# The run-out of an attention and adapter kernel, reordered: banks, additions and the branch at the end

## The chip, the cores and the metric

The kernel runs on one core of one Trainium2 chip. Its time is that of one execution on the device, in microseconds. The median of three runs of the kernel before the change is 412.86 us, the lowest 411.19 and the highest 413.30.

A core has five engines with an instruction stream each. TensorE (PE in the profile, PEld for its weight loads) multiplies matrices into PSUM. VectorE (DVE) and ScalarE (ACT) read PSUM and SBUF. GpSimd (POOL) works here on SBUF operands alone. SyncE (SP) issues transfers. Each engine runs its instructions strictly in the order of the program, and engines wait for one another by semaphores. Transfers can be issued from SP's, ScalarE's and GpSimd's queues.

## The reference

A spatial-reduction attention is followed by a mixture of low-rank adapters. Cut to what matters:

```python
# kv (4, 384, 32, 128), q (4, 12288, 128)
kv_pool = kv.reshape(B, H//4, 4, W//4, 4, C).mean(axis=(2, 4))   # 768 pooled rows per batch
k = v = kv_pool.reshape(B, -1, C) @ w_sr
a = softmax(q @ k.T / sqrt(C))
x = a @ v                                  # then seen as (49152, 128)

logits = x @ w_gate                        # 8 experts
topk = the two largest of the 8
w = softmax(logits[topk])
out = x + sum over the two of w * ((x @ A[e]) @ B[e])     # A: 128x16, B: 16x128
```

## The kernel before, in words

The 49152 tokens are cut into 96 chunks (`NCH`) of 512 tokens (`NTOK`), 24 chunks to each of the four batches. A chunk's tokens are handled as four groups (`NS`) of 128. The last chunk, 95, is called n in the code.

A chunk c goes through these helpers, each of which issues its instructions where it is called:

- `scores` (L231): on TensorE, 512 queries against two blocks of 128 keys, in a two-bank PSUM tile from the pool `ps_s` (`stile`, L147, two such tiles that take turns). ScalarE takes the exponential into `tt`. Three calls make a chunk.
- `weigh` (L242): the weighted sum of the values, 12 matmuls in each of two halves, into the two-bank tile `xps` of the pool `ps_x`, of which there is one. The value matrix has the 8 gate columns and a column of ones appended, so logits and the softmax's denominator come out with it.
- `normalise` (L253): on VectorE, a reciprocal, the multiplication that makes `xn` in SBUF and frees `xps`, and four searches for the largest logits.
- `gate` (L269) and `gate_weights` (L284): for a pair of chunks, the argument and the mask of the two best experts, and the weights by a tanh on ScalarE. The engine of the small multiplications and additions is a parameter, GpSimd or VectorE.
- `transposed` (L291): on TensorE, the transposes of x of one chunk (`cx`) and of the gated hidden values `hg` of an older one (`ch`) into one bank. It returns `evacuate`, which copies both to SBUF on VectorE or, with `True`, on ScalarE.
- `down` (L326): x times A into a bank `h_ps`. `apply_gate` (L332): on VectorE, `hg`, the product of it with the gate weights.
- `up` (L343): `hg` times B into a bank `d_ps`. With `plus_x` the same bank first takes x, by four fp32 matmuls with the identity (8 passes, L347).
- `give` (L353): VectorE adds `xn` to `d_ps` (L358), or, where x is in the bank already, ScalarE copies it (L356). Then the transfer of the 512 rows to the output is issued, from SP's queue unless another is named.

`mtile` takes a tile of the pool `ps_h`, which is one bank; `ps_t` is one bank too. With two for `ps_x` and four for `ps_s` all eight banks of PSUM are in use.

The order is written out by hand (`manual_schedule`). The main loop (L457) handles in its step c the scores of chunks c+1 and c+2, the weighted sum of c-1, the transposes of c-2 and c-4, `down` of c-3, and `up` and `give` of c-6. Pooling and keys of the next batch are spread over the steps (`prep`). From step 89 on, small pieces check that all values were in a safe range; `count_sum` (L394) adds up counts over partitions with a matmul into a bank of `ps_h`.

After the loop, from L505, comes the run-out for the chunks still on their way. The score pool is closed, and its four banks become the pool `ps_e`, named by `bank(0)` to `bank(3)`. The lines L511 to L557 are the order of the work there, each engine taking its own instructions out of it in that order. `tail_ok` (L401) and `all_ok` (L406) finish the check and leave a flag `bad`.

At the end each engine loads the flag into a register (`values_load`, L559), and an `If` (L562) holds a slow general version of the whole computation, which is not entered with these inputs. In the profile, L562 also names the waits for outstanding work that follow the branch, and L673 the closing steps of the program.

Of the kernel before, what the change touches and what calls it, by code (L numbers as in the profile page):

```python
# [21 lines left out]
def kernel(  # L22
# [44 lines left out]
    def mtile(shape, dtype=FP32, name="hd"):  # L67
        return ps_h.tile(shape, dtype, tag="hd", name=name)
# [78 lines left out]
    def stile(name):  # L147
        return ps_s.tile([P, 2, NTOK], FP32, tag="sg", name=name)
# [90 lines left out]
            mm(sg[:, k], kfT[b][:, j * P:(j + 1) * P], qc, start=True, stop=True)  # L239
        nc.scalar.activation(tt[c][:, 2 * r:2 * r + 2], sg, AF.Exp, bias=0.0, scale=scale)  # L240

    def weigh(c, h):  # L242
        b = c // CPB
        if h == 0:
            xps[c] = ps_x.tile([P, 2, 512], FP32, tag="x", name="xps")
        for j in range(h * NH, (h + 1) * NH):
            for s in range(NS):
                o = xps[c][:, s // 2, (s % 2) * VW:(s % 2 + 1) * VW]
                mm(o, tt[c][:, j, s::NS], vext[b][:, j],  # L249
                   start=(j == 0 and s % 2 == 0), stop=(j == NJ - 1 and s % 2 == 1),  # L250
                   skip_group_check=True)

    def normalise(c):  # L253
        ri = rinv_all[:, c]
        xv = xps[c][:, :, 0:2 * VW].rearrange("p b (s v) -> p b s v", v=VW)
        nc.vector.reciprocal(ri.rearrange("p (b s) -> p b s", b=2), xv[:, :, :, VW - 1])  # L256
        if c % 2 == 0:
            xpair[c // 2] = xpool.tile([P, 2 * NS, VW], FP32, tag="xn", name="xn")
        xn[c] = xpair[c // 2][:, (c % 2) * NS:(c % 2 + 1) * NS]
        nc.vector.tensor_tensor(  # L260
            xn[c].rearrange("p (b s) v -> p b s v", b=2), xv,
            ri.rearrange("p (b s) -> p b s", b=2).unsqueeze(3).broadcast_to([P, 2, 2, VW]),
            op=ALU.mult)
        if c % 2 == 0:
            gin[c // 2] = small.tile([P, 2 * NS, 8], FP32, tag="top", name="top")
        for s in range(NS):
            nc.vector.max(gin[c // 2][:, (c % 2) * NS + s], xn[c][:, s, C:C + E])  # L267
# [23 lines left out]
    def transposed(cx, ch, bank=None):  # L291

        if bank is None:
            t_ps = ps_t.tile([P, 2, NS, P], BF16, tag="tp", name="t_ps")
        else:
            t_ps = bank.bitcast(BF16).rearrange("p (k s c) -> p k s c", k=2, s=NS)
        todo = []
        if chunk_ok(cx):
            hi = xn[cx].bitcast(U16)[:, :, 1:2 * C:2].bitcast(BF16)
            todo += [(0, s, hi[:, s]) for s in range(NS)]  # L300
        if chunk_ok(ch):
            todo += [(1, s, hg[ch][:, s]) for s in range(NS)]
        if not todo:
            return lambda act=False: None
        for i, (k, s, src) in enumerate(todo):
            mm(t_ps[:, k, s], src, id_bf, is_transpose=True,  # L306
               start=(i == 0), stop=(i == len(todo) - 1), skip_group_check=True)

        def evacuate(act=False):
            xh = run.tile([P, 2, NS, P], BF16, tag="xh", name="xh", bufs=5)  # L310
            lo, hi_ = todo[0][0], todo[-1][0] + 1
            if act:
                nc.scalar.activation(xh[:, lo:hi_], t_ps[:, lo:hi_], AF.Copy)
            else:
                nc.vector.tensor_copy(xh[:, lo:hi_], t_ps[:, lo:hi_])  # L315
            if lo == 0:
                xT[cx] = xh[:, 0]
            if hi_ == 2:
                hgT[ch] = xh[:, 1]

        return evacuate

    def as_tokens(bank):
        return bank.rearrange("p (s c) -> p s c", s=NS)

    def down(c, bank=None):  # L326
        hps[c] = mtile([P, NS, P], name="h_ps") if bank is None else as_tokens(bank)
        for s in range(NS):
            mm(hps[c][:, s], xT[c][:, s], a_bf, start=(s == 0), stop=(s == NS - 1))  # L329
# [9 lines left out]

    dps = {}  # L340

    def up(c, bank=None, plus_x=False):

        dps[c] = mtile([P, NS, P], name="d_ps") if bank is None else as_tokens(bank)
        if plus_x:
            for s in range(NS):
                mm(dps[c][:, s], id_f32, xn[c][:, s, 0:C], start=(s == 0), stop=False,  # L347
                   skip_group_check=True)
        for s in range(NS):
            mm(dps[c][:, s], hgT[c][:, s], b_bf, start=(s == 0 and not plus_x),  # L350
               stop=(s == NS - 1), skip_group_check=True)

    def give(c, act=False, queue=None):  # L353
        osb = run.tile([P, NS, P], FP32, tag="osb", name="osb", bufs=8)
        if act:
            nc.scalar.activation(osb, dps[c], AF.Copy)  # L356
        else:
            nc.vector.tensor_tensor(osb, dps[c], xn[c][:, :, 0:C], op=ALU.add)  # L358
        t0 = c * NTOK
        (queue or nc.sync).dma_start(  # L360
            out[t0:t0 + NTOK, :].rearrange("(p s) c -> p s c", p=P), osb)
# [30 lines left out]
        nc.vector.tensor_scalar(flags[:, 2:], vmax, V_LO, None, op0=ALU.is_ge)  # L392

    def count_sum():  # L394
        cnt_ps = mtile([1, 2 + 2 * B], name="cnt_ps")
        mm(cnt_ps, ones_c, flags, start=True, stop=True)
        nc.vector.tensor_copy(cnt[:, 0:2], cnt_ps[:, 0:2])
        nc.vector.tensor_scalar(cnt[:, 2:], cnt_ps[:, 2:], 1.0, None, op0=ALU.min)  # L398
        nc.vector.tensor_reduce(tot, cnt, axis=AX.X, op=ALU.add)
# [57 lines left out]
    for c in range(1, NCH - 1):  # L457
        b, k = divmod(c, CPB)
        todo = [(c + 1, 2), (c + 2, 0), (c + 2, 1)]

        def next_scores():
            x, r = todo.pop(0)
            if x < NCH:
                scores(x, r)

        cs = c + 2
        if cs < NCH and cs % GRP == 0:
            g = cs // GRP
            if g + 2 < NQ:
                load_q(g + 2)  # L470
            if g + 3 < NQ:
                cast_q(g + 3)
        next_scores()
        if c >= 3 and c % 2 == 1:
            gate_weights((c - 3) // 2, nc.gpsimd)
        weigh(c - 1, 0)
        next_scores()
        if chunk_ok(c - 6):
            up(c - 6)
            give(c - 6)  # L480
        weigh(c - 1, 1)
        normalise(c - 1)
        if c % 2 == 0:
            gate(c // 2 - 1, nc.gpsimd)
        evacuate = transposed(c - 2, c - 4)
        next_scores()
        if b + 1 < B:
            prep(b + 1, k)
        if c == 1:
            ranges(0)  # L490
        a = slice(0, CUT * NS)
        if CUT < c <= CUT + 3:
            count_ok(a, c - CUT - 1, flags[:, 0:1])
        elif c == CUT + 4:
            values_ok()
        elif c == CUT + 5:
            count_sum()
        if chunk_ok(c - 3):
            down(c - 3)
            apply_gate(c - 3)  # L500
        evacuate(c == NCH - 2)
# [2 lines left out]

    score_banks.close()  # L505
    ps_e = ctx.enter_context(tc.tile_pool(name="ps_e", bufs=1, space=bass.MemoryType.PSUM))

    def bank(i):
        return ps_e.tile([P, NTOK], FP32, tag=f"e{i}", name=f"e{i}")

    n = NCH - 1  # L511
    gate_weights(n // 2 - 1, nc.gpsimd)
    weigh(n - 1, 0)
    weigh(n - 1, 1)
    normalise(n - 1)
    evacuate = transposed(n - 2, n - 4, bank(0))
    evacuate(True)
    down(n - 3, bank(1))
    apply_gate(n - 3)
    up(n - 6, bank(2))  # L520
    weigh(n, 0)
    weigh(n, 1)
    give(n - 6)
    normalise(n)
    tail_ok()
    gate(n // 2, nc.vector)
    evacuate = transposed(n - 1, n - 3)
    evacuate(True)
    down(n - 2)
    apply_gate(n - 2)  # L530
    up(n - 5, bank(3), plus_x=True)
    evac_x = transposed(n, NCH, bank(0))
    gate_weights(n // 2, nc.vector)
    evac_x(True)
    down(n - 1, bank(1))
    give(n - 5, act=True)
    up(n - 4, bank(2), plus_x=True)
    apply_gate(n - 1)
    evacuate = transposed(NCH, n - 2)
    evacuate(True)  # L540
    down(n)
    apply_gate(n)
    give(n - 4, act=True)
    end = ps_x.tile([P, 2, 512], FP32, tag="x", name="end")
    up(n - 3, end[:, 0], plus_x=True)
    give(n - 3, act=True)
    up(n - 2, bank(3), plus_x=True)
    evac_1 = transposed(NCH, n - 1, bank(0))
    evac_1()
    all_ok(bank(2))  # L550
    evac_2 = transposed(NCH, n, ps_t.tile([P, NTOK], FP32, tag="tp", name="t_ps"))
    evac_2()
    give(n - 2, act=True)
    up(n - 1, bank(1))
    give(n - 1, queue=nc.scalar)
    up(n)
    give(n, queue=nc.scalar)  # L557

    bad_v = nc.values_load(bad, min_val=0, max_val=1)  # L559


    with tc.If(bad_v != 0):  # L562
        b_full = const.tile([P, P], FP32)
        nc.vector.tensor_copy(b_full, b_f)
        big = kvpool.tile([P, 4 * 1024], FP32, tag="kvt", name="g_kv")
# [112 lines left out]
```

## Time and profile before

| | us |
|---|---|
| profiled execution, its own time | 412.09 |
| its span, from the first to the last instruction | 410.3 |
| median of three runs | 412.86 |
| TensorE busy | 380.0 |
| VectorE busy | 344.4 |
| ScalarE busy | 297.9 |
| GpSimd busy | 165.2 |
| end of the last computation (VectorE L358) | 403.73 |

All starts are counted from the start of the span. A busy TensorE is not TensorE at its peak, because matmuls overlap and their ends are modelled. The granted clock of TensorE has a mean of 0.991. The main loop's step takes 3.5 to 4.1 us near its end: step 94 is the stretch from 387.30 to 390.03 and the wait after it. The run-out's computation goes from 390.6 to 403.7.

A line of an engine's work has the line of the code, the engine, the operation, what is written from what, and the shape. "PEldq", "SPq" and the like are the sequencers of those engines, with the register, branch and issuing instructions that are not counted as busy. A chain is a list of pieces in order of time: start, length, and the engine and line that held up the end in that piece.

### The profile page before, as it was taken

The page shows a single profiled execution, that of the slowest core. Times are in us where ns is not written, and L with a number is a line of the kernel's source. Part 1 is how long each engine was busy: PE and PEld are TensorE (multiplying, and loading weights), DVE is VectorE, ACT ScalarE, POOL GpSimd, SP SyncE. Part 2 cuts the span into 40 slices and gives each one's busy share as a digit, 9 for nine tenths or more (in the row PEclk, how much of TensorE's full clock was granted, in tenths as well). Part 3 has the DMA queues.
Part 4 walks back from the last instruction along what each step waited for, and adds up shares of the span by engine and source line. Part 5 has one row for each costly group of instructions (what it writes and reads, how often), then busy time and mean ns, then how long its engine had stood idle before and what let it go on. Part 6 is the DMA issues. An engine that isn't in the chain of part 4 may idle for free.

```text
span 410.3 us, 11470 instructions
## 1 busy us (share of the span) xinstructions
PE 380.0 (93%) x4561; PEld 304.0 (74%) x4561; DVE 344.4 (84%) x969; ACT 297.9 (73%) x356; POOL 165.2 (40%) x315
## 2 busy tenths in 40 slices
PE   0659999999999999999999999989999999999992
PEld 0426888777877888877877888867878788787791
DVE  3663789898899989898899989898898989899982
ACT  1267888876687877876687878866777888877751
POOL 1020498882212487792212488692212212122120
PEclk9998999999999999999999999999999999999998
DMA  8999699797186999797186999797185474221123
GB/s 259 378 251 181 232 248 289 284 185 154 66 169 134 290 244 310 241 249 156 60 173 119 322 233 305 263 227 154 55 180 115 139 162 129 79 78 74 57 80 135
DMA packets 71372, 76.51 MB, mean 186 GB/s; under 512 B 51744, under 2 KB 52000, under 8 KB 70944
## 3 DMA queue, kind: packets, MB, share of 16 engines
q1 hardware_dynamic: 68816, 62.93, 55.1%
q0 software_dynamic: 736, 12.06, 16.8%
q10 hardware_dynamic: 1760, 0.73, 0.7%
q8 instruction: 37, 0.61, 0.6%
q14 instruction: 23, 0.19, 0.1%
HBM read 50.53 MB, written 37.22 MB: 214 GB/s over the span
## 4 chain that ended last, share of the span: by engine, by line
PE 79%; DMA 8%; DVE 7%; issue 2%; ACT 1%; ACTq 0%; SPq 0%; DVEq 0%; POOL 0%
PE xps L249 31%; PE sg L239 26%; PE t_ps L306 9%; PE d_ps L350 5%; PE h_ps L329 4%; DMA qT<-q_bf 3%; DMA b_f<-in_moe_B_dram 3%; DMA kvt<-in_kv_dram 2%; DVE xn L260 2%; DVE hg L334 2%; DMA q_bf<-in_q_dram 1%; PE v_ps L171 1%; PE k_ps L164 1%; DVE osb L358 1%; ACT tt L240 1%
## 5 line engine op out<-in xcount | busy, mean ns | idle before, releaser
L240 ACT ACTIVATE tt<-sg 128x1024 f16<-128x1024 f32 x288 | 282.6, 1022 | 75.8 <-PE sg L239 75.3
L239 PE MATMUL sg<-qT,kfT 128*128 128x512 bf16 x576 | 172.3, 382 | 2.4 <-ACT kfT L186 1.0
L249 PEld LDWEIGHTS <-tt 128*128 128x128 f16 x2304 | 154.6, 113 | 23.7 <-DVE xn L260 2.1
L249 PE MATMUL xps<-vext,tt 128*128 128x137 f16 x2304 | 170.9, 224 | 0.6 <-DVE xn L260 0.4
L358 DVE TENSOR_TENSOR osb<-d_ps,xn 128x512 f32<-128x512 f32 x90 | 62.1, 689 | 17.7 <-PE d_ps L350 14.3
L273 POOL TENSOR_TENSOR m<-top 128x8 f32<-128x8 f32 x47 | 10.9, 232 | 157.5 <-DVE top L267 157.2
L260 DVE TENSOR_TENSOR xn<-xps,rinv_all 128x548 f32<-128x548 f32 x96 | 69.9, 728 | 3.3
L140 POOL TENSOR_TENSOR kvt<-kvt 128x1024 f32<-128x1024 f32 x27 | 64.0, 2372 | 4.3 <-PE sg L239 1.9
L334 DVE TENSOR_TENSOR hg<-h_ps,gw 128x512 bf16<-128x512 f32 x94 | 63.8, 678 | 0.4 <-PE h_ps L329 0.4
L315 DVE COPY xh<-t_ps 128x1024 bf16<-128x1024 bf16 (+1 forms) x93 | 62.4, 671 | 0.0
L239 PEld LDWEIGHTS <-kfT 128*128 128x128 bf16 x576 | 45.3, 98 | 5.7 <-issue 2.3
L350 PEld LDWEIGHTS <-xh 128*128 128x128 bf16 x384 | 29.2, 98 | 25.8 <-issue 5.6
L329 PEld LDWEIGHTS <-xh 128*128 128x128 bf16 x384 | 29.2, 98 | 21.0 <-issue 0.7
L267 DVE MAX8 top<-xn 128x8 f32<-128x8 f32 x384 | 36.0, 156 | 3.3
L350 PE MATMUL d_ps<-b_bf,xh 128*128 128x128 bf16 x360 | 34.8, 219 | 3.2 <-DVE hg L334 2.9
L329 PE MATMUL h_ps<-a_bf,xh 128*128 128x128 bf16 x376 | 36.3, 219 | 0.6 <-DVE cnt L398 0.6
L306 PE MATMUL t_ps<-id_bf,hg 128*128 128x128 bf16 x376 | 36.3, 219 | 0.0
L306 PE MATMUL t_ps<-id_bf,xn 128*128 128x128 bf16 x376 | 36.3, 219 | 0.0
L288 POOL TENSOR_SCALAR th<-th 128x64 f32<-128x64 f32 x47 | 17.4, 370 | 37.4 <-ACT th L286 37.4
L256 DVE RECIPROCAL rinv_all<-xps 128x4 f32<-128x4 f32 x96 | 17.5, 183 | 14.4 <-PE xps L249 11.5
L306 PEld LDWEIGHTS <-xn 128*128 128x128 bf16 x384 | 26.0, 98 | 0.0
L306 PEld LDWEIGHTS <-hg 128*128 128x128 bf16 x384 | 25.4, 98 | 0.1
(96 smaller groups left out, 207.4 us busy)
## 6 DMA issues: line engine op xcount, KB each, us to landing
kvt<-in_kv_dram SPq DMA_DIRECT2D x48, 512.0 KB, 7.2
out_dram<-osb SPq DMA_DIRECT2D x94, 256.0 KB, 3.0
q_bf<-in_q_dram POOLq DMA_DIRECT2D x23, 512.0 KB, 6.3
out_dram<-osb ACTq DMA_DIRECT2D x2, 256.0 KB, 3.7
qT<-q_bf SPq DMA_TRANSPOSE x23, 6.7
w_in<-in_w_sr_dram ACTq DMA_DIRECT2D x1, 64.0 KB, 2.0
a_f<-in_moe_A_dram ACTq DMA_DIRECT2D x1, 64.0 KB, 9.6
b_f<-in_moe_B_dram ACTq DMA_DIRECT2D x1, 64.0 KB, 10.3
```

The costliest lines, as they stand in the source:

```text
L140: eng.tensor_tensor(v[:, 0], v[:, 0], v[:, d], op=ALU.add)
L239: mm(sg[:, k], kfT[b][:, j * P:(j + 1) * P], qc, start=True, stop=True)
L240: nc.scalar.activation(tt[c][:, 2 * r:2 * r + 2], sg, AF.Exp, bias=0.0, scale=scale)
L249: mm(o, tt[c][:, j, s::NS], vext[b][:, j], start=(j == 0 and s % 2 == 0), stop=(j == NJ - 1 and s % 2 == 1), skip_group_check=True)
L260: nc.vector.tensor_tensor(xn[c].rearrange("p (b s) v -> p b s v", b=2), xv, ri.rearrange("p (b s) -> p b s", b=2).unsqueeze(3).broadcast_t ...
L267: nc.vector.max(gin[c // 2][:, (c % 2) * NS + s], xn[c][:, s, C:C + E])
L306: mm(t_ps[:, k, s], src, id_bf, is_transpose=True, start=(i == 0), stop=(i == len(todo) - 1), skip_group_check=True)
L315: nc.vector.tensor_copy(xh[:, lo:hi_], t_ps[:, lo:hi_])
L329: mm(hps[c][:, s], xT[c][:, s], a_bf, start=(s == 0), stop=(s == NS - 1))
L334: nc.vector.tensor_tensor(hg[c].rearrange("p s (e r) -> p (s e) r", r=RK), hps[c].rearrange("p s (e r) -> p (s e) r", r=RK), g.rearrange(" ...
L350: mm(dps[c][:, s], hgT[c][:, s], b_bf, start=(s == 0 and not plus_x), stop=(s == NS - 1), skip_group_check=True)
L358: nc.vector.tensor_tensor(osb, dps[c], xn[c][:, :, 0:C], op=ALU.add)
```

## The change

The loop and the run-out are rewritten in these places:

- `weigh` can be given its PSUM tile. In the run-out chunk 94's sum (n-1) gets two of the closed score pool's banks, from a pool `ps_y`, which is closed after `normalise(n - 1)` and followed by `ps_f` with two banks. Chunk 95's sum (n) keeps `xps`.
- `up` loses `plus_x`; `x_first` puts x into a bank by fp32 matmuls and is called for n-2 alone. Four chunks did that before (n-5, n-4, n-3, n-2).
- `give` has three ways: `"add"` (VectorE, as before), `"copy"` (ScalarE, where x is in the bank) and `"pool"` (ScalarE copies, and GpSimd adds `xn` in place). `"pool"` is used for n-6, n-5, n-4 and n-3. n-6 is now done in the loop's step 94, with `d_ps` in a score bank; the transfer of each is issued from SP after the GpSimd addition.
- `count_sum` moves from step 93 to step 94 and uses a score bank.
- The order of the run-out differs. `gate(n // 2)` stays on VectorE and comes after the transposes of n-1, `gate_weights(n // 2)` goes from VectorE to GpSimd. `apply_gate(n)`, its transposes and `up(n)` come ahead of those of n-1. Output n is issued from SP; n-2 and n-1 from ScalarE's queue.
- The `If` names its false side as the block that is preferred next in the code.

```diff
--- before.py
+++ after.py
@@ -239,9 +239,11 @@
             mm(sg[:, k], kfT[b][:, j * P:(j + 1) * P], qc, start=True, stop=True)
         nc.scalar.activation(tt[c][:, 2 * r:2 * r + 2], sg, AF.Exp, bias=0.0, scale=scale)
 
-    def weigh(c, h):
+    def weigh(c, h, banks=None):
         b = c // CPB
-        if h == 0:
+        if banks is not None:
+            xps[c] = banks
+        elif h == 0:
             xps[c] = ps_x.tile([P, 2, 512], FP32, tag="x", name="xps")
         for j in range(h * NH, (h + 1) * NH):
             for s in range(NS):
@@ -339,23 +341,30 @@
 
     dps = {}
 
-    def up(c, bank=None, plus_x=False):
-
-        dps[c] = mtile([P, NS, P], name="d_ps") if bank is None else as_tokens(bank)
-        if plus_x:
-            for s in range(NS):
-                mm(dps[c][:, s], id_f32, xn[c][:, s, 0:C], start=(s == 0), stop=False,
-                   skip_group_check=True)
+    def x_first(c, bank):
+
+        dps[c] = as_tokens(bank)
         for s in range(NS):
-            mm(dps[c][:, s], hgT[c][:, s], b_bf, start=(s == 0 and not plus_x),
+            mm(dps[c][:, s], id_f32, xn[c][:, s, 0:C], start=(s == 0), stop=False,
+               skip_group_check=True)
+
+    def up(c, bank=None):
+        fresh = c not in dps
+        if fresh:
+            dps[c] = mtile([P, NS, P], name="d_ps") if bank is None else as_tokens(bank)
+        for s in range(NS):
+            mm(dps[c][:, s], hgT[c][:, s], b_bf, start=(s == 0 and fresh),
                stop=(s == NS - 1), skip_group_check=True)
 
-    def give(c, act=False, queue=None):
+    def give(c, how="add", queue=None):
+
         osb = run.tile([P, NS, P], FP32, tag="osb", name="osb", bufs=8)
-        if act:
+        if how == "add":
+            nc.vector.tensor_tensor(osb, dps[c], xn[c][:, :, 0:C], op=ALU.add)
+        else:
             nc.scalar.activation(osb, dps[c], AF.Copy)
-        else:
-            nc.vector.tensor_tensor(osb, dps[c], xn[c][:, :, 0:C], op=ALU.add)
+        if how == "pool":
+            nc.gpsimd.tensor_tensor(osb, osb, xn[c][:, :, 0:C], op=ALU.add)
         t0 = c * NTOK
         (queue or nc.sync).dma_start(
             out[t0:t0 + NTOK, :].rearrange("(p s) c -> p s c", p=P), osb)
@@ -392,7 +401,7 @@
         nc.vector.tensor_scalar(flags[:, 2:], vmax, V_LO, None, op0=ALU.is_ge)
 
     def count_sum():
-        cnt_ps = mtile([1, 2 + 2 * B], name="cnt_ps")
+        cnt_ps = stile("cnt_ps")[0:1, 0, 0:2 + 2 * B]
         mm(cnt_ps, ones_c, flags, start=True, stop=True)
         nc.vector.tensor_copy(cnt[:, 0:2], cnt_ps[:, 0:2])
         nc.vector.tensor_scalar(cnt[:, 2:], cnt_ps[:, 2:], 1.0, None, op0=ALU.min)
@@ -479,6 +488,9 @@
             up(c - 6)
             give(c - 6)
         weigh(c - 1, 1)
+        if c == NCH - 2:
+            up(c - 5, stile("d_ps")[:, 0])
+            give(c - 5, "pool")
         normalise(c - 1)
         if c % 2 == 0:
             gate(c // 2 - 1, nc.gpsimd)
@@ -493,7 +505,7 @@
             count_ok(a, c - CUT - 1, flags[:, 0:1])
         elif c == CUT + 4:
             values_ok()
-        elif c == CUT + 5:
+        elif c == CUT + 6:
             count_sum()
         if chunk_ok(c - 3):
             down(c - 3)
@@ -504,62 +516,72 @@
 
     score_banks.close()
     ps_e = ctx.enter_context(tc.tile_pool(name="ps_e", bufs=1, space=bass.MemoryType.PSUM))
+    x_banks = ExitStack()
+    ps_y = x_banks.enter_context(tc.tile_pool(name="ps_y", bufs=1, space=bass.MemoryType.PSUM))
 
     def bank(i):
         return ps_e.tile([P, NTOK], FP32, tag=f"e{i}", name=f"e{i}")
 
+    def t_bank():
+        return ps_t.tile([P, NTOK], FP32, tag="tp", name="t_ps")
+
     n = NCH - 1
     gate_weights(n // 2 - 1, nc.gpsimd)
-    weigh(n - 1, 0)
+    weigh(n - 1, 0, ps_y.tile([P, 2, 512], FP32, tag="y", name="xps"))
     weigh(n - 1, 1)
     normalise(n - 1)
+    x_banks.close()
+    ps_f = ctx.enter_context(tc.tile_pool(name="ps_f", bufs=1, space=bass.MemoryType.PSUM))
+
+    def fbank(i):
+        return ps_f.tile([P, NTOK], FP32, tag=f"f{i}", name=f"f{i}")
+
     evacuate = transposed(n - 2, n - 4, bank(0))
     evacuate(True)
     down(n - 3, bank(1))
     apply_gate(n - 3)
-    up(n - 6, bank(2))
+    up(n - 5)
+    give(n - 5, "pool")
     weigh(n, 0)
     weigh(n, 1)
-    give(n - 6)
     normalise(n)
     tail_ok()
-    gate(n // 2, nc.vector)
     evacuate = transposed(n - 1, n - 3)
     evacuate(True)
     down(n - 2)
+    gate(n // 2, nc.vector)
+    evac_x = transposed(n, NCH, fbank(0))
+    evac_x(True)
+    end = ps_x.tile([P, 2, 512], FP32, tag="x", name="end")
+    x_first(n - 2, end[:, 0])
+    up(n - 4, bank(1))
     apply_gate(n - 2)
-    up(n - 5, bank(3), plus_x=True)
-    evac_x = transposed(n, NCH, bank(0))
-    gate_weights(n // 2, nc.vector)
-    evac_x(True)
-    down(n - 1, bank(1))
-    give(n - 5, act=True)
-    up(n - 4, bank(2), plus_x=True)
-    apply_gate(n - 1)
+    gate_weights(n // 2, nc.gpsimd)
+    down(n - 1, fbank(1))
+    give(n - 4, "pool")
+    down(n, fbank(0))
     evacuate = transposed(NCH, n - 2)
     evacuate(True)
-    down(n)
     apply_gate(n)
-    give(n - 4, act=True)
-    end = ps_x.tile([P, 2, 512], FP32, tag="x", name="end")
-    up(n - 3, end[:, 0], plus_x=True)
-    give(n - 3, act=True)
-    up(n - 2, bank(3), plus_x=True)
-    evac_1 = transposed(NCH, n - 1, bank(0))
-    evac_1()
-    all_ok(bank(2))
-    evac_2 = transposed(NCH, n, ps_t.tile([P, NTOK], FP32, tag="tp", name="t_ps"))
-    evac_2()
-    give(n - 2, act=True)
-    up(n - 1, bank(1))
+    up(n - 3, bank(0))
+    apply_gate(n - 1)
+    evac_0 = transposed(NCH, n, t_bank())
+    evac_0()
+    up(n - 2)
+    all_ok(mtile([P, NTOK], name="okc"))
+    give(n - 3, "pool")
+    evac_1 = transposed(NCH, n - 1, fbank(1))
+    evac_1(True)
+    up(n, fbank(0))
+    give(n)
+    give(n - 2, "copy", queue=nc.scalar)
+    up(n - 1)
     give(n - 1, queue=nc.scalar)
-    up(n)
-    give(n, queue=nc.scalar)
 
     bad_v = nc.values_load(bad, min_val=0, max_val=1)
 
 
-    with tc.If(bad_v != 0):
+    with tc.If(bad_v != 0, preferred_fallthrough_block=False):
         b_full = const.tile([P, P], FP32)
         nc.vector.tensor_copy(b_full, b_f)
         big = kvpool.tile([P, 4 * 1024], FP32, tag="kvt", name="g_kv")
```

## The prediction

> **What bounds the kernel now.** I read the page first, then the chain of the work that ended last, cut to the end, then what follows the last computation.
>
> ```profile
> span 410.3 us, 11470 instructions
> PE 380.0 (93%) x4561; PEld 304.0 (74%) x4561; DVE 344.4 (84%) x969; ACT 297.9 (73%) x356; POOL 165.2 (40%) x315
> ```
>
> TensorE bounds the long middle, which the change leaves as it is up to chunk 93. The change can only move what lies after about 386 us. There the chain reads (start, length, what):
>
> ```profile
> 386.90 0.04 DVE cnt L397
> 386.94 0.08 DVE cnt L398
> 387.02 0.05 issue
> 387.07 0.40 PE h_ps L329 x4
> ...
> 389.83 0.74 DVE xn L260
> 390.57 0.04 issue
> 390.62 1.66 PE xps L249 x24
> ...
> 395.62 0.95 PE e L347 x8
> ...
> 401.45 0.42 DVE xh L315
> ...
> 402.46 0.68 DVE osb L358
> ```
>
> Three things are to be seen. At 387 TensorE waits for the copies out of cnt_ps. At 390.62 and again at 393.30 the weighted sums wait for VectorE to empty their one PSUM tile. From 394.95 to 401.43 the chain never leaves TensorE, and four groups like the one at 395.62 (x added by fp32 matmuls, 0.95 us each) are in it.
>
> The computation ends at 403.73, and the span 6.6 us later. Four views tell why: the branch of the If (line 562) by engine, the output transfers issued from 397 to 403 us and those issued from 403 to 404.5, and the DMA rate in forty slices of 401.5 to 407 us.
>
> ```profile
> L562 PEldq COMPARE_BRANCH  x1: 4394/4394/4394, 403.4 to 403.4; - x1
> L562 SPq COMPARE_BRANCH  x1: 58/58/58, 403.1 to 403.1; - x1
> ```
> ```profile
> DMA to landing us min/median/max: 2.0/2.0/2.0
> ```
> ```profile
> DMA to landing us min/median/max: 3.2/3.7/4.2
> ```
> ```profile
> GB/s 313 387 357 402 357 90 0 0 104 402 357 402 357 268 15 0 0 60 149 372 387 298 387 328 417 417 492 268 119 60 30 60 60 119 30 15 0 15 0 15
> ```
>
> Outputs land in 2.0 us, but the last two in 3.2 and 4.2. Their data moved at about 400 GB/s until about 405.2, and then a trickle went on for 2 us. Counted by DMA engine, 12 of the 16 shares of the last output had landed by 405.88 and the sixteenth only at 407.96. In that time the instruction queues fetched five blocks of code, one of them 16 KB with 1.26 us on a single engine. TensorE's branch needed 4.4 us, the others' under 0.1 (and some 0.45 to their next instruction). SP waits for the sixteenth share at 407.96 and the span ends 2.35 us after it; TensorE was through at 408.05 and is not last.
>
> **The base.** The profiled execution took 412.09 us, 1.8 more than its span and 0.2% under the 412.86 median; I subtract from the median.
>
> **The change, step by step.** n is chunk 95. Durations are rows of this trace: 4 bf16 matmuls 0.22 us of TensorE's chain, a full weighted sum 1.48, four fp32 additions of x 0.95; 0.2 from the last issue to the reader; VectorE hg 0.68, xn 0.73, osb 0.67; ScalarE 1.02 for a 1024-wide copy, 0.59 for 512.
>
> The count (count_sum) goes to chunk 94's step and into a score bank. Its TensorE wait of 0.56 at 387.07 and about 0.3 of its own go from step 93; chunk 93's second half ends 0.8 us sooner, at 388.61. In step 94 it costs 0.2 on TensorE and 0.4 on VectorE ahead of hg(91).
>
> New in step 94: up(89), 0.22 on TensorE until 388.83; a ScalarE copy until 389.63; a GpSimd add. A GpSimd add of this shape has a row:
>
> ```profile
> L144 POOL TENSOR_TENSOR kvt<-kvt x9: 1275/1284/1290, 59.7 to 274.7; 128x512 f32<-128x512 f32 x9
> ```
>
> So it ends at 390.94. Queued behind it on GpSimd is the gate of chunks 92 and 93, ready only at 390.2; it starts at 390.97 (391.05 before). On SP the output of 89 leaves at 391 instead of 394.9, with nothing pending behind it.
>
> Chunk 94's sum gets its own banks. If these are the ones of up(89), they are free at 389.63, and TensorE, there at 389.72, goes on to 391.20. If they were those of the count, it would wait for VectorE until 390.8, 1.05 more. I take the first, since the score buffers alternate and an even number of takes comes before the last score.
>
> VectorE then has count, hg(91) to 391.48, recip and xn(94) to 392.43, hg(92) to 393.72. TensorE: transposes to 391.75, down(92), up(90), and chunk 95's sum from 392.19 to 393.67 (394.95 before). xn(95) is done at 394.83 (395.94 before).
>
> From here VectorE's gate ends at 395.97 and the tanh at 396.3. The two gate multiplications move to GpSimd: 0.37 and 0.32 with 0.08 ahead of each, to 397.16, where VectorE's rows have 0.18 and 0.23. GpSimd is free by then: add(90) 393.8 to 395.08, then tail_ok to 395.95. hg(95) ends 397.88, hg(94) 398.48. TensorE, with one x instead of four (2.85 us less), has its work done by 397 and now waits for hg(95): transposed at 397.93, copied by 398.80, up(95) 398.86, osb(95) 399.96. The branch of 94: transposed 398.77, ScalarE 399.57, up(94) 399.85, osb(94) 400.73. The last output is issued at 400.76, 3.0 us before the 403.76 of now. The late piece is no longer TensorE but the gate chain through ScalarE and GpSimd. If TensorE's order were kept and only the three groups dropped, the same chain would still set the end, so those 2.85 us are worth less than they measure.
>
> Three edits cost nothing. ScalarE copies 90 to 93 out of their banks as it did before, and its one new copy, of 89, lies in its idle 1.10 us ahead of the 390.06 transposed copy. The banks that chunk 94's sum gives back are free at 392.43 and first taken at 394.88; without those 2.4 us of cover the transpose of 95 would wait for xn(94). The check at the end (two small matmuls, 0.2, and two VectorE pieces, 0.4) fits between evac_0 and osb(95), which waits for up(95) until 399.29 anyway; if not, osb(95) and osb(94) come up to 0.4 later, still ahead of the transfers that are queued.
>
> GpSimd's add(91) runs 397.2 to 398.5 and add(92) to 399.85. SP issues output 92 at 399.9, and output 95, queued behind that wait, at 400.28; ScalarE issues 93 at 400.2 and 94 at 400.76. So 1 MB goes out at once. The first lands 2.0 us after 399.9, and each further 256 KB needs 0.62 to 0.70 us at 376 to 425 GB/s: the last lands at 403.9. This bunching costs 1.1 against an empty queue.
>
> [...]
>
> The branch with the untaken side next: if the code runs straight on, TensorE fetches nothing, no block of code lies ahead of the last output's shares, and nothing is added to 403.9. The tail of 2.35 us stays. New end: 403.9 + 2.35 = 406.25, 4.1 less than 410.33. Bounds of this step: the stragglers stay (2.1 more), or SP's pause of 0.4 us inside the tail goes too (0.4 less).
>
> Sum: 412.86 - 4.1 = 408.8.
>
> **Rivals.**
>
> The branch gives nothing (B). If the false side's code is next but ends in a jump of its own over the true side, the fetches and the stragglers stay: 2.1 back, and SP's 0.45 pause comes after the landing. Gain 1.5 to 2.0, time 410.9 to 411.4. For it: the waits of line 562 run before line 673's and something must lie between them. Against it: now there is one branch per engine and no second jump.
>
> That jump is slow on SP (E, slower). As B, but SP's target is not loaded: TensorE's 4.39 us, now after the last landing. 403.9 + 2.1 + 4.39 + 2.35 = 412.7, 2.4 later than now: 415.3. It decides when SP's jump costs over 4.0 us. Against it: SP's branch now costs 0.06 and 0.47 to the next instruction.
>
> Chunk 94's sum waits for the count's copies (C): all that follows is 1.05 later, gain 3.05, time 409.8.
>
> GpSimd becomes the bound (D): if its strided x makes an add as dear as the 128x1024 row, 2.37, then add(92) ends at 402.7 and output 95 issues behind it at 403.1: last landing 405.4, gain 2.6, time 410.3. Against: all nine 512-wide rows are within 15 ns.
>
> **How the numbers follow.** The text's case has 0.52, and its own range is 407.4 to 409.9 (0.7 us either way on the last issue, the DMA rate, SP's 0.4). B has 0.22, C 0.10, D 0.06, E 0.10. Within 0.5% (2.06 us, about what a measurement of this kernel can tell from no change) lie two thirds of B and a fifth of E. Faster: 0.52 + 0.10 + 0.06 + 0.07 = 0.75; same 0.15 + 0.02 = 0.17; slower 0.08. The range takes the text's case, C, D and B with half a microsecond over its end: 406.8 to 411.9.
>
> **What would show it.** Right: four L140-like GpSimd adds near 1.28 us; four groups of fp32 additions gone to one; chunk 95's sum starting near 392.2; last output issued near 400.8; TensorE's branch under 0.5 us; last landing near 404. Wrong: a 4 us branch still there or a second jump; a wait of xps for cnt; output 95 late behind add(92); a weighted-sum wait that stays at 0.4 us. Wrong altogether if the early steps of the loop differ, which nothing here touches.

## The result, and the profile after

The changed kernel is slower by 0.43%: the ratio to the kernel before is 1.0043, with a 95% interval of 1.0026 to 1.0061 (20 runs of each, medians 413.19 and 411.68 us). The predicted time was 408.8, with a range of 406.8 to 411.9.

The head of the page of the kernel after:

```profile
span 410.5 us, 11440 instructions
PE 378.4 (92%) x4537; PEld 302.0 (74%) x4537; DVE 342.3 (83%) x965; ACT 298.8 (73%) x358; POOL 170.5 (42%) x321
```

Every engine's busy time but ScalarE's and GpSimd's went down, as the diff makes one expect. What happened in the run-out is in the timeline of the kernel after (start, length, engine, line, instructions, and in brackets the idle time before them with what ended it):

```profile
384.78 0.59 PE L239 MATMUL sg<-qT,kfT 128*128 128x512 bf16 x2
...
388.30 0.20 PE L405 MATMUL cnt_ps<-flags,ones_c 128*1 128x10 f32 x2
...
388.64 1.18 POOL L367 TENSOR_TENSOR osb<-osb,xn 128x512 f32<-128x512 f32 x1 [4.06 <-ACT osb L365]
...
389.13 0.77 DVE L279 TENSOR_TENSOR msk<-xn,top 128x64 f32<-128x64 f32 x1
...
389.89 0.14 DVE L407 TENSOR_SCALAR cnt<-cnt_ps 1x8 f32<-1x8 f32 x1
...
390.19 1.62 PE L251 MATMUL xps<-vext,tt 128*128 128x137 f16 x24 [1.35 <-DVE cnt L407]
...
392.53 1.62 PE L251 MATMUL xps<-vext,tt 128*128 128x137 f16 x24
...
397.48 2.35 POOL L367 TENSOR_TENSOR osb<-osb,xn 128x512 f32<-128x512 f32 x2
397.53 1.29 DVE L336 TENSOR_TENSOR hg<-f,gw 128x512 bf16<-128x512 f32 x2 [0.59 <-POOL gw L291]
...
400.57 0.69 DVE L363 TENSOR_TENSOR osb<-d_ps,xn 128x512 f32<-128x512 f32 x1 [0.17 <-PE d_ps L356]
400.60 1.04 ACTq L369 DMA_DIRECT2D out_dram<-osb  x2
```

The first line is the second score pair of step 93, up to which both kernels do the same work. It stands at 385.79 us in the profile before and at 384.78 here. These 1.01 us are a difference between two executions, so I count from this mark. Three readings: chunk 94's sum waits 1.35 us for the count's copies. These are late because the mask ahead of them took 0.77 instead of 0.23. And all the computation ends at 401.27, 16.5 us after the mark, where it was 17.9 (403.73 against 385.79).

So the computation is 1.5 us shorter, and the time is longer. The branch, by engine, in the kernel after:

```profile
L584 PEldq COMPARE_BRANCH  x2: 90/2452/4813, 400.7 to 401.0; - x2
L584 SPq COMPARE_BRANCH  x2: 38/43/48, 401.8 to 406.4; - x2
```

There are now two branches per engine, and the second of TensorE takes 4.81 us. On SP eight waits (L584, 402.0 to 406.3 us) stand between the first branch and the second, and behind the second stands L695, the closing steps. The listing of the built program has the same order: behind the branch comes the false side, then the true side, then the program's end, and the false side closes with a jump to the end. On SP that false side holds the waits for the outputs, so its jump comes after the last landing, at 406.37. SP's line asked for from 406 to 409 us, and the closing steps of the program on SP:

```profile
L584 SPq COMPARE_BRANCH  x1: 38/38/38, 406.4 to 406.4; - x1
```
```profile
L695 SPq EVENT_SEMAPHORE  x13: 17/28/28, 408.9 to 409.9; - x13
```

Between the jump at 406.37 and the next instruction at 408.89 lie 2.5 us in which SP does nothing. Two blocks of code are fetched in that pause, one of 16 KB from 406.58 and one of 8 KB from 407.30. Last, the output transfers issued from 399 us on, and the DMA rate in forty slices of 399 to 407:

```profile
DMA to landing us min/median/max: 2.0/3.3/4.7
```
```profile
GB/s 0 0 143 399 369 369 31 0 215 379 389 369 389 399 338 307 430 348 359 420 348 461 51 82 20 61 10 0 10 10 10 31 10 0 0 0 0 82 0 0
```

The bulk has moved by 403.5, and the trickle of the kernel before is there again: one of the sixteen shares of the last output landed at 406.02, the other fifteen by 404.56.

### The profile page after: what moved, and what is told of

Read it like the earlier page. It is cut to its first block, busy times and chain, and to the rows that moved or that the text cites. A ratio compares the mean times of both kernels' runs of the same rounds, so it can differ in the third digit from the quotient of the medians.

```text
span 410.5 us, 11440 instructions
## 1 busy us (share of the span) xinstructions
PE 378.4 (92%) x4537; PEld 302.0 (74%) x4537; DVE 342.3 (83%) x965; ACT 298.8 (73%) x358; POOL 170.5 (42%) x321
## 4 chain that ended last, share of the span: by engine, by line
PE 79%; DMA 9%; DVE 6%; issue 2%; ACT 1%; POOL 1%; ACTq 0%; SPq 0%; POOLq 0%
PE xps L251 31%; PE sg L239 27%; PE t_ps L308 9%; PE d_ps L356 5%; PE h_ps L331 4%; DMA b_f<-in_moe_B_dram 3%; DMA qT<-q_bf 3%; DMA kvt<-in_kv_dram 2%; DMA q_bf<-in_q_dram 1%; DVE hg L336 1%; DVE xn L262 1%; PE v_ps L171 1%; PE k_ps L164 1%; ACT tt L240 1%; DVE vmax L197 1%
## 5 line engine op out<-in xcount | busy, mean ns | idle before, releaser
L363 DVE TENSOR_TENSOR osb<-d_ps,xn 128x512 f32<-128x512 f32 x90 | 62.1, 690 | 17.9 <-PE d_ps L356 14.4
L356 PEld LDWEIGHTS <-xh 128*128 128x128 bf16 x384 | 29.1, 98 | 24.5 <-issue 4.2
L308 PEld LDWEIGHTS <-xn 128*128 128x128 bf16 x384 | 25.9, 98 | 0.5 <-DVE xn L262 0.5
```

Of the source, the lines that this page charges most:

```text
L308: mm(t_ps[:, k, s], src, id_bf, is_transpose=True, start=(i == 0), stop=(i == len(todo) - 1), skip_group_check=True)
L356: mm(dps[c][:, s], hgT[c][:, s], b_bf, start=(s == 0 and fresh), stop=(s == NS - 1), skip_group_check=True)
```

## The experiments

Each kernel's run-out is taken apart into three legs, from the records of its profile: from the mark to the issue of the last output, from there to the last landing, and from there to the end. They don't hold what ran before the mark. That part differs by up to 2.8 us between the profiled executions, and also between two of the same kernel. Ratios are to the kernel before, run on the same chip in the same session.

| kernel | to last issue | to landing | tail | sum, us | ratio (95%) |
|---|---|---|---|---|---|
| before | 17.97 | 4.20 | 2.37 | 24.5 | 1 |
| after | 16.52 | 4.72 | 4.53 | 25.8 | 1.0043 (1.0026 to 1.0061) |
| after, measured again (e11) | 16.50 | 4.75 | 4.64 | 25.9 | 1.0034 (1.0013 to 1.0055) |
| order only (e1) | 16.51 | 4.76 | 2.35 | 23.6 | 1.0017 (0.9996 to 1.0037) |
| order only, measured again (e10) | 16.51 | 4.69 | 2.35 | 23.6 | 0.9973 (0.9948 to 0.9998) |
| option only (e2) | 17.98 | 4.61 | 4.58 | 27.2 | 1.0084 (1.0063 to 1.0106) |
| after, short jump (e3) | 16.51 | 4.24 | 1.20 | 22.0 | 0.9963 (0.9945 to 0.9982) |
| before, short jump (e4) | 17.98 | 4.22 | 1.20 | 23.4 | 0.9983 (0.9963 to 1.0004) |
| after, no If (e5) | 16.51 | 2.66 | 1.18 | 20.4 | 0.9909 (0.9876 to 0.9942) |
| order, count moved (e6) | 15.29 | 4.93 | 2.35 | 22.6 | 0.9962 (0.9934 to 0.9991) |
| e6, gate first (e7) | 14.99 | 5.01 | 2.35 | 22.4 | 0.9938 (0.9911 to 0.9965) |
| e7, short jump (e8) | 14.99 | 4.65 | 1.20 | 20.8 | 0.9924 (0.9894 to 0.9954) |
| e7, rolled (e9) | 15.00 | 4.64 | 1.20 | 20.8 | 0.9936 (0.9911 to 0.9961) |

My theory after the result: the branch option costs some 2 us by SP's jump, the reordering gains, and the code fetched at the jump delays the last shares. The rival: the reordering itself, with its GpSimd additions and its outputs in one bunch, is what costs.

### Order and option apart

The order alone, the changed kernel with

```diff
-    with tc.If(bad_v != 0, preferred_fallthrough_block=False):
+    with tc.If(bad_v != 0):
```

> The changed kernel without its branch option: only the reordered run-out. Theory (the false side's own jump costs SP 2.5 us after the last landing, and the reordering itself is a gain): the tail after the last landing is 2.3 us again instead of 4.5, the ratio to the kernel before is 0.994 to 0.998, some 2 us under the changed kernel. Rival (the reordering, with its GpSimd adds and bunched outputs, is what costs): the ratio stays at 1.003 to 1.006.

and the option alone, the kernel before with the opposite edit:

> The kernel before with the branch option alone. Theory: TensorE's long branch stays, the straggling shares of the last output stay, and SP gets a second jump after the last landing that takes about 2.5 us: ratio 1.004 to 1.006. Rival (the option is neutral or a gain): 0.997 to 1.001.

The option alone costs 0.84%, more than I expected, and its tail is 4.58 us, the same as the changed kernel's. Its branches in the profile:

```profile
L562 SPq COMPARE_BRANCH  x2: 38/43/48, 403.3 to 408.9; - x2
L562 PEldq COMPARE_BRANCH  x2: 90/2322/4553, 403.6 to 403.9; - x2
```

It shortens nothing: TensorE's long branch is still there, at 4.55 us, and SP's jump is put behind the last landing at 408.55. The order alone was not the clear gain that I expected: 1.0017, where its legs promise 0.9 us less. All four kernels of that session (e1 to e4) lay 0.4 to 1.6 us above their legs, so their common reference may have run low. I measured it again, with the changed kernel beside it:

> A second look at the changed kernel without its branch option, on the chip of this call. By the profiles (last issue 1.5 us sooner, landing 0.5 later, same tail) it should be 0.9 us under the kernel before, ratio 0.996 to 0.999. Rival (something that the profiles do not show takes the reordering's gain): 1.001 to 1.004 as in the first look.

> The changed kernel itself beside the two others on the same chip. Theory: 2.1 us (0.5%) over the same order without the option, ratio to the kernel before 1.002 to 1.006. Rival: no difference from the order without the option.

This time the order alone is 0.9973 and the changed kernel 1.0034: 2.5 us between the two medians of one session (412.81 and 410.31), where the tails differ by 2.3. So the rival falls: it is the option, not the reordering, that makes the changed kernel slower. Whether the order alone gains is less sure. Its legs (0.9 us) and the second measurement (0.9948 to 0.9998) say so, the first (0.9996 to 1.0037) does not.

### How far the jump goes

The general version in the true side is four copies, one per batch. Counted in the built program they are 218 instructions on TensorE and 151 on SP. Cut to one copy they are 56 and 46:

```diff
-        for b in range(B):
+        for b in range(1):
```

> The changed kernel whose general version, in the side that is not entered, covers batch 0 only (batches 1 to 3 of it are left out, so the jump is over about a quarter of the code). Theory (distance makes the fetch): TensorE's branch under 1 us, SP's jump about 0.5 us, no fetch among the last outputs, the last landing 2 us earlier; ratio to the kernel before 0.988 to 0.993. Rival (the straggling shares of the last output are the outputs' own bunching, and the jump's price does not depend on distance): landing as late as before, ratio 1.002 to 1.006.

> The kernel before, with the general version in the side that is not entered cut to batch 0 (batches 1 to 3 of it left out). Theory: the last output lands 2.1 us after its issue instead of 4.2, ratio 0.994 to 0.996. Rival: no change, 0.999 to 1.001.

In both, TensorE's branch falls to 0.30 and 0.34 us, and the tail to 1.20. The changed kernel with a short jump is 0.37% under the kernel before. TensorE's price goes with the code that is passed in these runs: 4.4 to 4.9 us over 218 instructions in eight profiles, 0.30 to 0.35 over 56 or 82 in four.

For SP the runs do not show that. Shortening the general version also took six of SP's eight waits out of the false side. First the kernel after, then the same with the short jump (e3):

```profile
L584 SPq EVENT_SEMAPHORE  x8: 17/17/17, 402.0 to 406.3; - x8
```
```profile
L584 SPq COMPARE_BRANCH  x2: 38/43/48, 401.7 to 402.0; - x2
L584 SPq EVENT_SEMAPHORE  x2: 17/17/17, 401.8 to 401.9; - x2
```

The waits for the outputs now come behind SP's jump, which stands at 401.98, 3.5 us ahead of the last landing. There its price, 0.47 us to the next instruction, adds nothing to the end. In e4, where SP has no second jump, the same shift of the waits takes 1.17 us off the tail. So of the 3.3 us that the tail lost in e3, about 1.2 belong to the waits and 2.2 to the place of the jump. Why fewer waits stand there, no run shows.

Nor does the number of instructions explain the 2.5 us. SP's branch in the kernel before passes the same 151 instructions, and its next instruction comes 0.47 us later; over 46 (e4) it is 0.46. What makes SP's jump slow in the changed kernel stays open. In all three profiles of the option with the long general version (after, e11, e2) the pause is 2.5 to 2.6 us and one 8 KB block is fetched in it.

The last landing did not move by the 2 us that I expected, 4.24 after the last issue in e3 and 4.22 in e4, and so both ratios lie above my ranges. One block of 16 KB is still fetched beside the last outputs (at 403.0 and 405.7), and again one share comes about 1.2 us behind the fifteenth. So I left the If out:

> The changed kernel without the flag's loads, the If and the general version (left out altogether; the computed check stays). Theory (code fetched at the branch slows single DMA engines under the last outputs): no 16 KB fetch between 401 and 405, all sixteen shares of the last output land within 0.3 us of each other, 2.6 to 2.9 us after its issue instead of 4.7; ratio to the kernel before 0.985 to 0.991. Rival (four outputs at once make the late shares): the last share still 4 us or more after its issue, ratio 0.992 to 0.997.

Transfers issued from 403 to 404.5 us, and the rate from 401.7 to 409.7, without the If:

```profile
DMA to landing us min/median/max: 2.2/2.7/2.7
```
```profile
GB/s 0 0 82 399 389 369 72 0 174 369 358 410 379 369 420 348 358 430 369 359 420 369 113 0 0 0 0 0 0 0 0 0 0 0 0 0 0 0 0 0
```

The same four outputs (1 MB) go out at the same rate, and then there is nothing: no trickle and no fetch, and the sixteen shares of the last output land within 0.21 us. The bunching of four outputs costs 0.66 us over a lone output's 2.0; the other 2.1 us of the changed kernel's 4.72 go with the If and the code fetched for it.

### The wait for the count, and the held mask

> The reordered run-out without the branch option, and the count's matmul and VectorE copies moved from step 94 to the run-out, after hg(93), into the unused half of the last sum's tile. Theory (the new banks of chunk 94's sum are those of the count, and its 1.35 us wait is a real loss): that sum starts 1.2 us sooner against step 93, the last output is issued 0.7 to 1.0 us sooner; ratio to the kernel before 0.996 to 0.999, 0.7 us or more under the run without the move. Rival (VectorE or the gate chain is late anyway): the last issue moves by less than 0.3 us.

```diff
-    def count_sum():
+    def count_sum(bank):
-        cnt_ps = stile("cnt_ps")[0:1, 0, 0:2 + 2 * B]
+        cnt_ps = bank[0:1, 0:2 + 2 * B]
...
-        elif c == CUT + 6:
-            count_sum()
...
     apply_gate(n - 2)
+    count_sum(end[:, 1])
```

The wait is gone (chunk 94's sum starts right behind down(91)), and the last issue comes 1.22 us sooner, more than I expected. So the banks that the sum had waited for were the count's, not those of up(89). The mask remains long in this kernel:

```profile
391.03 1.19 POOL L367 TENSOR_TENSOR osb<-osb,xn 128x512 f32<-128x512 f32 x1 [4.06 <-ACT osb L365]
...
391.52 0.78 DVE L279 TENSOR_TENSOR msk<-xn,top 128x64 f32<-128x64 f32 x1
```

It ends at 392.30, 0.08 after the GpSimd addition. Then the gate goes first:

> As the run with the count moved, and in step 94 the gate of chunks 92 and 93 is issued ahead of the GpSimd addition for chunk 89 (and of its ScalarE copy). Theory (VectorE's mask, with two SBUF inputs, is held until a GpSimd addition that runs at the time has ended): the mask of that step takes 0.23 us instead of 0.77, hg(91) comes 0.5 us sooner, the last issue moves 0.2 to 0.5 us. Rival (the mask's length in that step has another cause): it stays over 0.5 us.

```diff
             up(c - 5, stile("d_ps")[:, 0])
-            give(c - 5, "pool")
         normalise(c - 1)
         if c % 2 == 0:
             gate(c // 2 - 1, nc.gpsimd)
+        if c == NCH - 2:
+            give(c - 5, "pool")
```
```profile
391.26 0.23 DVE L279 TENSOR_TENSOR msk<-xn,top 128x64 f32<-128x64 f32 x1
...
392.13 1.19 POOL L367 TENSOR_TENSOR osb<-osb,xn 128x512 f32<-128x512 f32 x1
```

The same mask takes 0.23, with the addition behind it, and the last issue moves by 0.30. This kernel computes all that the kernel before does, and is 0.62% faster. Next, the same with the cut general version:

> As the run with the gate first, and the general version in the side not entered cut to batch 0 (batches 1 to 3 of it left out). Theory: the gains of the order (1.5 us, and 1 more for the two moves) and of the short jump (1.2 us of tail, 0.5 of landing) add up: ratio to the kernel before 0.988 to 0.992. Rival (the outputs' bunching takes the order's gain back): 0.994 to 0.997.

By the legs the gains add up, 20.8 us against 22.4 of the run with the gate first. The ratio, 0.9924 (0.9894 to 0.9954), is a little over the range that I expected, and the times alone can't tell the two runs apart.

### A version that keeps everything

The general version can be short without being cut: a loop over the batches at run time, instead of four copies.

```diff
         for b in range(B):
+            nc.vector.tensor_copy(kp_all[:, b * NKV:(b + 1) * NKV], kpT[b])
+        with tc.For_i(0, B) as bi:
+            nc.vector.tensor_copy(kp.unsqueeze(1), kp_all.rearrange("p (b k) -> p b k", b=B)[:, bass.ds(bi, 1)])
...
-            with tc.For_i(b * N, (b + 1) * N, P) as t0:
+            with tc.For_i(0, N, P) as t0:
```

> As the run with the gate first, and the general version kept whole but rolled: a loop over the four batches around the loop over tokens, in place of four copies of the code. Theory (what counts is how much code the jump passes): TensorE's branch under 1 us, tail after the last landing about 1.2 us, ratio to the kernel before 0.988 to 0.994, like the run whose general version was cut to batch 0. Rival (the jump's price is of another kind): 0.9925 to 0.996 like the run with the gate first, with a TensorE branch of over 4 us.

```profile
L584 PEldq COMPARE_BRANCH  x1: 350/350/350, 401.2 to 401.2; - x1
L584 SPq COMPARE_BRANCH  x1: 58/58/58, 402.4 to 402.4; - x1
```

Now 82 instructions on TensorE and 79 on SP are passed. TensorE's branch takes 0.35 us; SP's takes 0.06, as in the kernel before, and again only two of its waits stand at the branch. The legs are those of the cut version, 3.7 us under the kernel before, and the ratio is 0.9936 (0.9911 to 0.9961). By the times alone it can't be told from the run with the gate first. The legs say 1.5 us: 1.15 in the tail, where the waits moved, and 0.37 in the landing.

> The rolled general version with the If's condition turned, so that the general side is entered and computes the whole output a second time: 384 passes of its loop, an estimated 20 us each by some 60 operations of 0.2 to 0.7 us in a row and two transfers of 2 us, 5 to 15 ms in all. It tells what the side costs that is jumped over; no theory of the change hangs on it.

That one run took 8941 us in all, some 8500 more than the kernel without the general side (TensorE's granted clock had a mean of 0.555 in it). It is a side that should not be entered, and its code is worth keeping small.

## Why the prediction was wrong

The readings of the kernel before held. One small sum did not: 0.8 us off the 389.59 at which chunk 93's second half ended is 388.8, not 388.61 (on the same clock the kernel after has 388.73). It does not decide. The sum of the three legs was predicted to fall by 4.1 us and rose by 1.2. Term by term:

- "The branch with the untaken side next: if the code runs straight on" failed first. It does not: the false side ends in a jump over the true side (two branches per engine, SP's at 401.8 and 406.37), which was the mechanism of rivals B and E. Against B I had put that there was one branch per engine and no second jump, against E that SP's branch costs 0.06 us and 0.47 to the next instruction. Both told of the old layout only. What B took as 0.45 us on SP and E as 4.39 measured 2.5: the tail grew from 2.37 to 4.53, 2.2 us. That this jump has such a price is shown (after against e1 and e10, e2 against before); why it has it is not, and no run shows whether SP's target was loaded, as E supposed.
- In the same step, "no block of code lies ahead of the last output's shares" failed with it: 2.1 us, by the run without the If.
- "If these are the ones of up(89)" chose the wrong one of two cases that the step itself had priced: rival C was true. I had argued from the order in which score buffers are taken and from a guess of how the new pools lie on the old ones, which no row of the profile shows. The wait was 1.35, where 1.05 was priced. A step that was not in the prediction at all made the copies later: the mask held behind the GpSimd addition, 0.77 us instead of 0.23. Together they kept the last issue at 16.5 after the mark. With both taken away (e7) it is 14.99, and the gain on the kernel before 2.98, against the 3.0 of the prediction. That nearness is in part luck, since e7 has the count in another place than the prediction. The kernel after itself is the better witness: from the start of chunk 95's sum to the last issue the prediction has 8.57 us (392.19 to 400.76), the profile 8.76 (392.53 to 401.29). So that part of the replay was right to 0.2 us, with the gate chain as the new bound.
- The bunching was priced too high: 3.14 from the last issue to the last landing, where 2.66 was measured without code fetches. That is 0.5 us to the good.

-4.1 + 2.2 + 2.1 + 1.5 - 0.5 is 1.2, what the legs show. The ratio makes 1.77 us (1.07 to 2.51), and 1.2 lies in that.

What was right: SP's outputs behind the GpSimd additions were no bound (output 92 was issued at 399.85 and 95 at 400.42, ahead of ScalarE's two); GpSimd's adds took 1.18 where 1.28 was taken from the contiguous row (VectorE's took 0.69, but GpSimd's lay beside other work); TensorE stopped being the bound of the run-out. What the adds cost came by another way, the held mask (0.77 us in place of 0.23).

The chance of 0.32 for B and E together was too small for a step on which nothing in the trace bore, and B and E were priced without C; two rivals that hold at once were given no time.

## What to carry to other kernels

The side of a branch that was laid out next was not free of a jump here (two branches per engine in place of one): ask where such a side goes when it ends, and what stands in front of that jump. Here it held the waits for the last outputs, and its jump was added to the end (2.2 us). The last outputs landed 2.1 us later with the branch and the code fetched at it than without. TensorE's branch took 0.35 us over 82 instructions and 4.4 to 4.9 over 218, so keep the code that is passed over short, and then see where the waits have gone (1.2 us of the tail in e4). A bank handed on within a schedule brought its last reader with it (a wait of 1.35 us), and the reader was late for a reason of its own, so name the reader before giving the wait no cost.

## What the runs showed of the hardware

**VectorE's mask, with both inputs in SBUF, was held by a two-input GpSimd addition that was under way.** In the kernel before, the mask's 48 rows go from 0.22 to 1.99 us, and I had not asked why. The long one, in VectorE's timeline and in GpSimd's:

```profile
267.89 1.99 DVE L277 TENSOR_TENSOR msk<-xn,top 128x64 f32<-128x64 f32 x1
```
```profile
264.98 4.82 POOL L140 TENSOR_TENSOR kvt<-kvt 128x1024 f32<-128x1024 f32 x2 [1.93 <-PE sg L239]
```

The second addition ends at 269.80, the mask at 269.88. In every long case of both profiles (0.55 to 1.99 us, with the 0.77 of step 94 among them) the mask ends 0.08 us after the addition beside it. VectorE's operations hg, with one input from PSUM, are not held: the two at 397.53 take 1.29 together while two additions run on GpSimd until 399.83. So the mask was held for the whole rest of the addition, 0.54 us of it in step 94. What holds it no row shows, and the prediction gave it no time.

**Code is fetched beside the outputs, and some outputs beside a fetch land late.** A block of 16 KB took 0.9 to 1.6 us in the profiles before and after, and in every kernel with the branch one share of the last output landed 1.0 to 2.0 us behind the fifteenth (1.14 in the kernel before, 1.46 in the kernel after); without the branch all sixteen lay within 0.21. The loop says the same. In the kernel before, a 16 KB block was under way beside 39 of the 96 outputs, and 14 of them had a last share over 0.8 us behind the fifteenth; of the 57 others none had. In the kernel after it is 16 of 36 and 2 of 60. (Beside means from 1.2 us after the issue to the landing of the fifteenth share.) Whether the late share is that of the DMA engine that fetches is not shown. TensorE's branch took 4.4 to 4.9 us where 218 instructions were passed and 0.3 where 56 were. SP's pass over 151 took 0.47 us to the next instruction in the kernel before and 2.5 in the changed one, so the number of instructions alone does not say what a jump costs.

**Open.** With the short jump one 16 KB block of code is still fetched beside the last outputs, and one share is late by more than a microsecond. How to have that fetch earlier or later was not tried. Why SP's jump over the same instructions takes 2.5 us in one layout and 0.47 in the other was not tried either. Why the first measurement of the order alone lay 1.6 us over its legs, where the second lay within 0.2, is not settled; the two profiles are alike.
